# Two whole-row buffers for h in PSUM, borrowed by every other visitor of that memory

## The chip, the cores and the metric

The kernel runs on one core of one Trainium2 chip. Its time is the device time of one launch in microseconds (us), as a median of several runs. Five engines take part: TensorE (PE) multiplies, VectorE (DVE) and ScalarE (ACT) read what PE leaves in PSUM, GpSimd (POOL) works on SBUF alone, and SyncE (SP) issues every DMA. Each engine runs its own list of instructions in the order in which the program was written; it stops at an instruction whose semaphores have not come, and everything behind that instruction on the same engine stops with it.

## The reference

```python
def _attn_ref(x, inducing):                 # x: 4 x 12608 x 128, inducing: 32 x 128
    def mab(q, kv):
        s = scale * (q @ kv.transpose(0, 2, 1))
        s = s - s.max(-1, keepdims=True)
        a = np.exp(s)
        a /= a.sum(-1, keepdims=True) + 1e-09
        return a @ kv
    h = mab(I, x)                           # per batch: 32 rows out of 12608
    return mab(x, h)                        # and back: 12608 rows
def _moe_ref(x, w_in, w_out, g_ln):         # x: 50432 x 128, w_in: 128 x 1024, w_out: 1024 x 128
    h = x @ w_in
    sm = softmax of h over its 1024 columns
    solu = h * sm
    ln = (solu - mean) / np.sqrt(var + 1e-06) * g_ln
    return ln @ w_out
```

All inputs and outputs that the kernel moves are float32, but w_in and w_out, which come as float64 and are rounded on the chip.

## The kernel before, in words

Each of the four batches is cut into 99 tiles of up to 128 rows, 396 in all. The first attention needs all rows of a batch before its result exists, so the program has two passes.

**Pass 1** (`p1`, nine groups of up to 12 tiles per batch) loads rows, turns them on PE (L561, a visit of up to 4 tiles each), copies the turned rows to SBUF on ACT (L547) and stores them for pass 2. It then computes scores (L589), their maxima (DVE L605, PE L614), exponentials (ACT L639) and a weighted sum of the rows (PE L665, "gather"). `combine` closes a batch: the sum of weights (L707), the 32 mean rows (L714), and their product with w_in (L726), kept in SBUF as `hs`.

**Pass 2** (`p2`) loads the turned rows, computes scores against the 32 rows (L768) and turned weights `aT` (L804). `main` then makes each tile's hidden row block `h` = `aT` times `hs` (L902): 128 x 1024 float32, which is two of PSUM's eight banks. The text calls this **mm1**. `soft` follows: DVE scales h, takes its minimum and moves it to SBUF (L940); ACT takes the exponential (L950); POOL multiplies (L954); ACT squares (L965); DVE turns blocks of 32 x 32 (L978). Four tiles make a group. `products` multiplies a group with w_out (L1023); `evacuate` moves the result out of PSUM on DVE or ACT (L1045); `finish` scales the rows (ACT L1100 or POOL L1096) and stores them.

PE's row groups are used apart. The products of a group come as two streams, each of which keeps two of the four row groups busy. A **beat** is one step of PE: both streams side by side (full), one stream and one step of mm1 side by side (full), or one of the three alone (half). mm1 is four beats; one stream is 32.

PSUM before: two banks for h, one buffer alone; two each for the two streams (`op0`, `op1`); one bank `tr` for the turns and scores of `p2` and the turns of `p1`; one bank `pb` for `p1`'s scores and sums. Batch 0's pass 1, the early phase, has nothing beside it and borrows the banks of `op` and h.

The order on every engine comes from a planner in the program (`Planner`), which runs while the program is built. Every operation has a cost in ns and a priority; `AFTER` has the latency between two engines; `Lock` hands out buffers to the tasks that wait, the most urgent first. `driver` emits products in PE's spare time, `JC` beats at a time, and a stream joins if it will be ready within `EAGER` ns. `SWITCH` is what the planner adds for a visit to another use of PE. Where the planner sees PE idle for more than `FILL` ns it writes dummy transposes (L488).

Of the kernel before, what the change touches and what calls it, by code (L numbers as in the profile page):

```python
# [11 lines left out]
U32 = mybir.dt.uint32  # L12
# [17 lines left out]
JC = 1  # L30
BEAT = 225
EAGER = 60
SWITCH = 170


def cut(total, most, unit):
# [28 lines left out]
PR_EV = -60
PR_FI = 20
PR_G2 = 6
PR_HN = -2
PR_MU = -1
PR_SQ = 1.5  # L70
PR_TU = 3
RUSH = -100.0
SLACK = {"PE": 100, "ACT": 0, "DVE": 300, "POOL": 0, "SP": 0}
SPARE = 150
WARM = 32
WOUT = -13.5

AFTER = {
    "PE": {"PE": 0, "ACT": 197, "DVE": 196, "POOL": 200, "SP": 250},
    "ACT": {"PE": 205, "ACT": 143, "DVE": 142, "POOL": 61, "SP": 50},  # L80
    "DVE": {"PE": 256, "ACT": 128, "DVE": 127, "POOL": 155, "SP": 50},
    "POOL": {"PE": 205, "ACT": 75, "DVE": 74, "POOL": 100, "SP": 50},
    "SP": {"PE": 1036, "ACT": 1000, "DVE": 920, "POOL": 1000, "SP": 1000},
# [27 lines left out]
class Lock:  # L111


    def __init__(self, bufs=()):
        self.free = [(b, ()) for b in bufs]
        self.waiting = []


class Planner:
# [18 lines left out]
    def give(self, lock, buf, *after):  # L138
        lock.free.append((buf, after))
        while lock.free and lock.waiting:  # L140
            lock.waiting.sort(key=lambda w: (w[0][1], w[1]))
            task, _ = lock.waiting.pop(0)
            self.blocked -= 1
            self._step(task, lock.free.pop(0))

    def _step(self, task, value):
        gen = task[0]
        while True:
# [90 lines left out]
def set_attention_then_solu_kernel(ctx: ExitStack, tc: tile.TileContext, x, inducing, w_in, w_out, g_ln, out):  # L239
# [21 lines left out]
    psum = pool("psum", 1, PSUM)  # L261
# [29 lines left out]
    op_b = [buf([P, 2, 512], f"op{w}", where=psum) for w in range(2)]  # L291
    op_e = [o[:, i, :] for o in op_b for i in range(2)]
    early_h = tc.tile_pool(name="h_early", bufs=1, space=PSUM, side="right")
    where = early_h.__enter__()
# [8 lines left out]
    H, VT, XN, XT, TRB, PB = (Lock() for _ in range(6))  # L303
# [8 lines left out]
    OS = Lock(bufs(2, [P, GS, C], "os"))  # L312
# [126 lines left out]
    def weights_in():  # L439
        g = yield from rounded(w_in_sb, w_in.bitcast(U32), conv, None, conv_free, -18.5)  # L440
        plan.set(w_in_ready, g)

    def weights_out():
# [30 lines left out]
        give(TRB, mp, d)  # L474
        rows = wc.rearrange("p (k q) d -> p k q d", q=4)
        spread = []
        for a in range(4):
            for q in range(4):
                c = yield dma(
                    M * FF * 4,  # L480
                    lambda: nc.sync.dma_start(rows[a * M : (a + 1) * M, :, q, :C], wg[q * M : (q + 1) * M]), d, issue=600, prio=LATE,
# [10 lines left out]
    def points():  # L492
        def warm():
# [8 lines left out]
        give(TRB, tr_b, d)  # L502
        plan.scratch = (TRB, PB, H)
# [8 lines left out]
    EARLY_X = Lock([spare[:, i * each : (i + 1) * each].rearrange("p (s c) -> p s c", c=C) for i in range(SPARES * FF // each)] + xn_b[:1])  # L512
    EARLY_T = Lock([vt_all[:, i * each : (i + 1) * each].rearrange("p (s t) -> p s t", t=P) for i in range(3 * GS * FF // each)] + [xT_b])
    e2 = xn_b[1].rearrange("p s c -> p (s c)")
    EARLY_EW = Lock([(e2[:, i * 2 * PG * M : (i * 2 + 1) * PG * M], e2[:, (i * 2 + 1) * PG * M : (i + 1) * 2 * PG * M].rearrange("p (s m) -> p s m", m=M)) for i in range(2)] + [ew_b])
    EARLY_TR = Lock(op_e[:3])
    EARLY_PB = Lock([*h_e, pb_b, op_e[3]])
# [3 lines left out]
    def p1(b, k):  # L521
# [4 lines left out]
        lx, lt, ltr, lpb, lew = (EARLY_X, EARLY_T, EARLY_TR, EARLY_PB, EARLY_EW) if early else (XN, XT, TRB, PB, EW)  # L526
# [16 lines left out]

        def copy(c0, c1, tr, d):
# [679 lines left out]
```

## Time and profile before

| | |
|---|---|
| median of 3 runs | 1289.62 us (1284.67 to 1293.36) |
| the profiled execution | 1285.68 us, of which the span from first to last instruction is 1283.9 us |
| busy over the span | PE 97%, PE weight loads 87%, DVE 89%, ACT 89%, POOL 86% |
| granted TensorE clock | 0.992 on average |

A busy share counts the time in which at least one instruction of the engine was in flight. Matmuls overlap each other, so short gaps between them do not show in PE's share. The sum in the prediction is made against 1285.68 us; the median of the runs lies 3.94 us above it.

### The profile page before, as it was taken

The numbers are of one execution on the slowest core, as the hardware profiler recorded it, in microseconds if no ns is written. First come the engines' busy times: TensorE is split into PE (matmuls) and PEld (weight loads), VectorE is DVE, ScalarE is ACT, GpSimd is POOL, SyncE is SP. The second block draws the span as 40 slices with busy tenths as digits, with TensorE's granted clock in tenths as the row PEclk, the third lists the DMA queues.
The fourth block names the chain that finished last, engine by engine and source line by source line (L and its number), as shares of the span: only waits on it lengthen the run. The fifth ranks groups of instructions, "written<-read, shape, count | busy, mean of one in ns | idle before, by whom it ended". The sixth has DMA issues, their size and how long they took to land.

```text
span 1283.9 us, 75837 instructions
## 1 busy us (share of the span) xinstructions
PE 1246.2 (97%) x34221; PEld 1120.8 (87%) x34221; DVE 1140.8 (89%) x1825; ACT 1140.1 (89%) x2418; POOL 1104.2 (86%) x981
## 2 busy tenths in 40 slices
PE   8899999999999999999999999999999999999996
PEld 6689888889888888889888998888989999999996
DVE  5589989999898989999888999899999999999993
ACT  5489999999889989999789999989988999999993
POOL 2388988889889988988888997978889999999994
PEclk9999999999999999999899999999999999999998
DMA  9652333331232233332133134233021211111111
GB/s 361 188 164 70 111 103 94 93 111 43 77 117 60 78 102 119 103 109 74 28 102 94 43 103 138 91 101 102 21 82 54 58 55 53 54 38 43 29 29 41
DMA packets 118149, 113.46 MB, mean 88 GB/s; under 512 B 76577, under 2 KB 83777, under 8 KB 117697
## 3 DMA queue, kind: packets, MB, share of 16 engines
q1 hardware_dynamic: 117824, 108.62, 27.6%
q8 instruction: 267, 4.37, 1.4%
q14 instruction: 58, 0.47, 0.1%
HBM read 54.30 MB, written 52.18 MB: 83 GB/s over the span
## 4 chain that ended last, share of the span: by engine, by line
PE 70%; DVE 3%; ACT 2%; issue 1%; POOL 1%; POOLq 0%; DVEq 0%; ACTq 0%
PE op L1023 46%; PE h L902 15%; PE tr L561 2%; PE tr L804 2%; PE tr L768 1%; PE pb L665 1%; PE pb L589 1%; ACT sq L965 1%; DVE spare L940 1%; DVE vt L978 1%; ACT eu L950 1%; POOL eu L954 1%; PE pb L726 0%; DVE hn L940 0%; PE pb L614 0%
## 5 line engine op out<-in xcount | busy, mean ns | idle before, releaser
L1023 PE MATMUL op<-wc,vt 32*128 32x129 f32 x25600 | 1007.7, 275 | 12.5 <-issue 8.4
L1023 PEld LDWEIGHTS op<-wc,vt 32*128 32x128 f32 x25600 | 945.4, 185 | 54.3 <-issue 39.8
L902 PE MATMUL h<-hs,aT 32*128 32x128 f32 x6336 | 442.8, 277 | 3.2 <-DVE spare L940 1.2
L902 PEld LDWEIGHTS h<-hs,aT 32*128 32x128 f32 x6336 | 387.9, 187 | 32.1 <-DVE spare L940 6.2
L954 POOL TENSOR_TENSOR eu<-spare,eu 128x1024 f32<-128x1024 f32 x144 | 341.2, 2376 | 33.8 <-ACT eu L950 33.4
L954 POOL TENSOR_TENSOR eu<-hn,eu 128x1024 f32<-128x1024 f32 x140 | 331.8, 2376 | 25.1 <-ACT eu L950 24.3
L978 DVE STREAM_TRANSPOSE vt<-eu 128x1024 f32<-128x1024 f32 x284 | 349.2, 1233 | 1.1 <-POOL eu L954 0.9
L965 ACT ACTIVATE sq<-eu 128x1024 bf16<-128x1024 f32 x284 | 298.9, 1053 | 17.2 <-POOL eu L954 13.7
L940 DVE TENSOR_SCALAR_CACHE_REDUCE hn<-h,rn 128x1024 f32<-128x1024 f32 x198 | 252.1, 1273 | 38.8 <-PE h L902 30.6
L940 DVE TENSOR_SCALAR_CACHE_REDUCE spare<-h,rn 128x1024 f32<-128x1024 f32 x198 | 251.8, 1272 | 37.2 <-PE h L902 28.2
L950 ACT ACTIVATE eu<-hn,nm 128x1024 f32<-128x1024 f32 x140 | 160.3, 1145 | 19.9 <-DVE hn L940 19.0
L950 ACT ACTIVATE eu<-spare,nm 128x1024 f32<-128x1024 f32 x144 | 164.9, 1145 | 10.7 <-DVE spare L940 10.5
L954 POOL TENSOR_TENSOR spare<-hn,spare 128x1024 f32<-128x1024 f32 x58 | 137.5, 2374 | 15.6 <-ACT spare L950 15.5
L954 POOL TENSOR_TENSOR spare<-spare 128x1024 f32<-128x1024 f32 x54 | 128.0, 2373 | 16.9 <-ACT spare L950 16.4
L978 DVE STREAM_TRANSPOSE vt<-spare 128x1024 f32<-128x1024 f32 x112 | 138.2, 1235 | 0.0
L965 ACT ACTIVATE sq<-spare 128x1024 bf16<-128x1024 f32 x112 | 117.7, 1051 | 9.3 <-POOL spare L954 8.3
L1100 ACT ACTIVATE os<-spare,fin 128x128 f32<-128x128 f32 (+1 forms) x276 | 86.9, 391 | 1.5 <-POOL fin L1085 1.2
L950 ACT ACTIVATE spare<-hn,nm 128x1024 f32<-128x1024 f32 x58 | 66.4, 1145 | 6.7 <-DVE hn L940 6.4
L1045 DVE COPY spare<-op 128x258 f32<-128x258 f32 (+1 forms) x123 | 50.2, 416 | 24.6 <-PE op L1023 23.6
L950 ACT ACTIVATE spare<-spare,nm 128x1024 f32<-128x1024 f32 x54 | 61.9, 1146 | 6.5 <-DVE spare L940 6.5
L965 ACT ACTIVATION_READ_ACCUMULATOR sq<-eu 128x1 f32 x284 | 54.2, 191 | 0.0
L561 PE MATMUL tr<-ident,xn 128*128 128x128 f32 x297 | 48.8, 287 | 0.4 <-DMA xn<-in_x_dram 0.4
(180 smaller groups left out, 1028.0 us busy)
## 6 DMA issues: line engine op xcount, KB each, us to landing
out_dram<-os SPq DMA_DIRECT2D x96, 256.0 KB, 2.4
xT<-xd SPq DMA_DIRECT2D x27, 768.0 KB, 4.6
xn<-in_x_dram SPq DMA_DIRECT2D x22, 768.0 KB, 5.4
xd<-xT SPq DMA_DIRECT2D x21, 768.0 KB, 4.3
dl<-dd SPq DMA_DIRECT2D x396, 1.0 KB, 2.4
xd<-vt SPq DMA_DIRECT2D x7, 768.0 KB, 10.6
spare<-in_x_dram SPq DMA_DIRECT2D x5, 768.0 KB, 10.3
xT<-xd SPq DMA_DIRECT2D x5, 512.0 KB, 4.2
```

The source lines that it names most:

```text
L561: nc.tensor.transpose(out=tr[:, (s - c0) * P : (s - c0 + 1) * P], in_=xn[:, s, :], identity=ident)
L589: nc.tensor.matmul(sc[g * M : (g + 1) * M, : nn * M], lhsT=indT, rhs=xT[:, :nn, g * M : (g + 1) * M], start=True, stop=True)
L804: nc.tensor.transpose(out=tr[:h, (q - q0) * P : (q - q0 + 1) * P], in_=a4[:, q * P : q * P + h], identity=ident)
L902: nc.tensor.matmul(hp[:, cols], lhsT=aT[rows, i // 2, :], rhs=hs[rows, cols], start=True, stop=True)
L940: lambda: nc.vector.tensor_scalar(out=hn, in0=hp, scalar1=rn, scalar2=None, op0=ALU.mult, op1=ALU.min, accum_out=nm),
L950: "ACT", 1133, lambda: nc.scalar.activation(e, hn, AF.Exp, bias=nm, scale=-1.0, accum_out=G["S"][:, s : s + 1]), d, rel, srel,
L954: d = yield Op("POOL", 2330, lambda: nc.gpsimd.tensor_tensor(out=e, in0=hn, in1=e, op=ALU.mult), de, prio=t + PR_MU)
L965: "ACT", 1040, lambda: nc.scalar.activation(sq, e, AF.Square, scale=1.0 / 32.0, accum_out=G["qe"][:, s, 0:1]), d,
L978: lambda: nc.vector.transpose(out=G["vtb"][:, : n * FF].rearrange("p (j s t) -> p j s t", j=M, s=n)[:, :, s, :], in_=e.rearrange("p (a f) ...
L1023: nc.tensor.matmul(op[:rows, a - 2 * w, : C + 1], lhsT=vt[q, k, :], rhs=wc[q, k, :], start=(k == 0), stop=(k == JB - 1))
L1045: return lambda: eng(F["raw"][:rows, i0 : i0 + 2, :], op[:rows, :, : C + 1])
L1100: nc.scalar.activation(os[:rows, q, :], raw[:, q, :], AF.Copy, scale=y[:, i0 + q : i0 + q + 1])
```

## The change

PSUM now holds two h buffers of two banks each, and the two stream buffers; `tr` and `pb` are gone. Turns, scores, sums of `p1` and `combine`, and the scores and turns of `p2`, each take one of the h buffers from the same lock for their visit and give it back. Since such a buffer is 1024 columns wide, late turns of `p1` go up to 6 tiles a visit instead of 4, those of `p2` up to 8 column blocks instead of 4, and `combine`'s product with w_in is one visit instead of two. The `p1` score visit gives its buffer back after the exponentials, and the gather takes one again.

The early phase has eight banks of its own, four for turns and four for scores, and more places for loaded rows, so that all nine groups of batch 0 have one. The h and stream buffers exist only when that phase and its `combine` are done. The planner's constants change: SWITCH 170 to 400, all latencies between engines in AFTER 80 ns longer, JC 1 to 2, EAGER 60 to 120, and the priorities.

```diff
-JC = 1
+JC = 2
-EAGER = 60
-SWITCH = 170
+EAGER = 120
+SWITCH = 400
+H_LAST = -30
-HN_MORE = 3
+HN_MORE = 4
-FILL = 1200
+FILL = 400
-P1_FROM = 0
-P1_GO = 20
-P1_STEP = 8
-P2_AHEAD = 29
+P1_FROM = 5
+P1_GO = -20
+P1_STEP = 7
+P2_AHEAD = 35
-PR_TU = 3
+PR_TU = 6
...
-    "PE": {"PE": 0, "ACT": 197, "DVE": 196, "POOL": 200, "SP": 250},
+    "PE": {"PE": 0, "ACT": 277, "DVE": 276, "POOL": 280, "SP": 330},
...
-    op_b = [buf([P, 2, 512], f"op{w}", where=psum) for w in range(2)]
-    h_e = [buf([P, 512], f"h_e{i}", where=where) for i in range(2)]
-    tr_b = buf([P, 512], "tr", where=psum)
-    pb_b = buf([P, 512], "pb", where=psum)
+    bank_e = [buf([P, 512], f"bank_e{i}", where=where) for i in range(8)]
...
-    EARLY_TR = Lock(op_e[:3])
-    EARLY_PB = Lock([*h_e, pb_b, op_e[3]])
+    EARLY_TR = Lock(bank_e[:4])
+    EARLY_PB = Lock(bank_e[4:])
...
-        lx, lt, ltr, lpb, lew = (EARLY_X, EARLY_T, EARLY_TR, EARLY_PB, EARLY_EW) if early else (XN, XT, TRB, PB, EW)
+        lx, lt, ltr, lpb, lew = (EARLY_X, EARLY_T, EARLY_TR, EARLY_PB, EARLY_EW) if early else (XN, XT, H, H, EW)
...
+        most = 4 if early else -(-n // 2)
-        for c0 in range(0, n, 4):
-            c1 = min(c0 + 4, n)
+        for c0 in range(0, n, most):
+            c1 = min(c0 + most, n)
...
+        if not early:
+            give(lpb, big, de)
+            big, rel = yield lpb
+        pooled = big[:, 512 - C : 512]
-        dp = yield Op("PE", 74 * n, gather, d)
+        dp = yield Op("PE", 74 * n, gather, d, rel)
...
-        for k in range(2):
-            spawn(half(slice(k * 512, (k + 1) * 512)), PRIO_P1(b, NP - 1))
+        for k in range(1 if b else 2):
+            spawn(half(FF if b else 512), PRIO_P1(b, NP - 1) if b else -28)
...
-        bank = EARLY_TR if b == 0 and j < ON_EARLY else TRB
+        bank = H
-        for q0 in range(0, -(-n // 2), 4):
-            q1 = min(q0 + 4, -(-n // 2))
+        for q0 in range(0, -(-n // 2), 8):
+            q1 = min(q0 + 8, -(-n // 2))
...
-            hp, rel = yield H
+            hp, rel = yield H.at(t + H_LAST)
...
+        bank_pool.__exit__(None, None, None)
+        late = pool("late", 1, PSUM, side="right")
+        for i in range(2):
+            give(H, buf([P, FF], f"h{i}", where=late), *done)
+        plan.scratch = (H,)
+        for w in range(2):
+            give(OP[w], buf([P, 2, 512], f"op{w}", where=late), *done)
```

On PE, in the steady part of the program, before (h_716 is the one h buffer, L902 is mm1, L1023 the products, L561 a turn visit of `p1` into its own bank `tr`):

```order
L1023 MATMUL op1_73<-wc_158,vt_68 128x129 x2
L902 MATMUL h_716<-hs1_126,aT0_95 128x128 x8
L1023 MATMUL op0_72<-wc_158,vt_68 128x129 x2
L1023 MATMUL op1_73<-wc_158,vt_68 128x129 x2
L561 MATMUL tr_79<-ident_139,xn1_71 128x128 x4
L1023 MATMUL op0_72<-wc_158,vt_68 128x129 x2
L1023 MATMUL op1_73<-wc_158,vt_68 128x129 x2
```

Every mm1 writes h_716, so it stands behind DVE's L940 of the tile before it. On PE with the change, one tile's mm1 into h1 and the next tile's into h0 (L924 is mm1, L1045 the products):

```order
L924 MATMUL h1_728<-hs1_125,aT1_96 128x128 x2
L1045 MATMUL op1_730<-wc_157,vt_65 128x129 x2
L924 MATMUL h0_727<-hs1_125,aT1_96 128x128 x2
L1045 MATMUL op0_729<-wc_157,vt_65 128x129 x2
L924 MATMUL h0_727<-hs1_125,aT1_96 128x128 x2
L1045 MATMUL op0_729<-wc_157,vt_65 128x129 x2
L924 MATMUL h0_727<-hs1_125,aT1_96 128x128 x4
L1045 MATMUL op1_730<-wc_157,vt_65 128x129 x12
L924 MATMUL h1_728<-hs1_125,aT1_96 128x128 x8
```

Here two mm1 stand back to back, and the third waits for the first one's buffer. Where a visit holds the other buffer, mm1 stays on one. On PE with the change, a turn visit of `p1` (L571, six tiles) into h0 beside mm1 on h1:

```order
L1045 MATMUL op0_729<-wc_157,vt_65 96x129 x2
L1045 MATMUL op1_730<-wc_157,vt_65 96x129 x2
L571 MATMUL h0_727<-ident_138,xn0_67 128x128 x6
L924 MATMUL h1_728<-hs0_123,aT1_96 128x128 x2
L1045 MATMUL op0_729<-wc_157,vt_65 96x129 x2
L924 MATMUL h1_728<-hs0_123,aT1_96 128x128 x2
```

The visit is longer by two tiles and its buffer comes from the lock of h. On PE at the end of the early phase, before (L665 the last gather, L464 the column means of w_out):

```order
L665 MATMUL h_e0_77<-spare_69,ew_100 32x128 x7
L464 MATMUL tr_79<-hn2_83,ones_mean_151 128x128 x8
L714 MATMUL h_e1_78<-fold_144,accn_137 128x128
L768 MATMUL op1_73<-xT2_87,h4_0_123 32x128 x4
L726 MATMUL pb_80<-w_in_sb_154,h4_0_123 128x512
L726 MATMUL op0_72<-w_in_sb_154,h4_0_123 128x512
L804 MATMUL op1_73<-ident_139,a4_94 128x128 x2
L902 MATMUL h_716<-hs0_124,aT0_95 128x128 x8
```

and with the change (L682 is the gather, L493 the dummy transposes, L731, L747, L790 and L826 what L714, L726, L768 and L804 were):

```order
L682 MATMUL bank_e4_76<-xn1_68,ew_99 32x128 x7
L493 MATMUL bank_e0_72<-ident_138 128x128 x14
L731 MATMUL bank_e2_74<-fold_143,accn_136 128x128
L493 MATMUL bank_e0_72<-ident_138 128x128 x6
L747 MATMUL bank_e3_75<-w_in_sb_153,h4_0_122 128x512
L747 MATMUL bank_e5_77<-w_in_sb_153,h4_0_122 128x512
L790 MATMUL h0_727<-xT2_86,h4_0_122 32x128 x4
L465 MATMUL h0_727<-hn2_82,ones_mean_150 128x128 x8
L826 MATMUL h0_727<-ident_138,a4_93 128x128 x2
L790 MATMUL h1_728<-xT2_86,h4_0_122 32x256 x4
L924 MATMUL h0_727<-hs0_123,aT0_94 128x128 x8
```

The product with w_in moved ahead of the first scores of pass 2, the means of w_out behind them, and 20 dummy transposes stand in the gap.

## Rows read from the trace of the kernel before

**Rows 1.** The page's first part: busy time, share of the span, instructions.

```profile
PE 1246.2 (97%) x34221; PEld 1120.8 (87%) x34221; DVE 1140.8 (89%) x1825; ACT 1140.1 (89%) x2418; POOL 1104.2 (86%) x981
```

**Rows 2.** Stages by windows: length, each engine's busy time (instructions), clock, DMA, GB/s.

```profile
core 0: us, PE busy (x) PEld busy (x) DVE busy (x) ACT busy (x) POOL busy (x), PEclk, DMA share, GB/s
70.00:1000.00 930.00, 913.48 (x25456) 815.88 (x25458) 853.60 (x1368) 853.23 (x1803) 821.33 (x713) 1.00 0.29 88
1000.00:1190.00 190.00, 186.98 (x5570) 175.60 (x5566) 178.50 (x251) 179.56 (x377) 183.82 (x165) 1.00 0.18 49
1190.00:1254.00 64.00, 64.00 (x1953) 62.18 (x1952) 59.84 (x76) 62.41 (x135) 62.81 (x54) 1.00 0.11 28
```

**Rows 3.** The chain that ended last: start, length, what.

```profile
1253.40 20.70 PE op L1023 x644
```

**Rows 4.** Timeline of one tile, 1231.0 to 1233.8 us: start, length, engine, line.

```profile
1231.07 0.38 PE L902 MATMUL h<-hs,aT 32*128 32x128 f32 x2
...
1231.28 0.28 PE L902 MATMUL h<-hs,aT 32*128 32x128 f32 x2
...
1231.97 1.84 PE L1023 MATMUL op<-wc,vt 32*128 32x129 f32 x58
1232.37 1.28 DVE L940 TENSOR_SCALAR_CACHE_REDUCE spare<-h,rn 128x1024 f32<-128x1024 f32 x1 [0.20 <-PE h L902]
...
1233.58 0.08 DVE L940 DVE_READ_ACCUMULATOR spare<-h,rn 128x1 f32 x1
...
1233.72 0.38 PE L902 MATMUL h<-hs,aT 32*128 32x128 f32 x2
```

**Rows 5.** Line L940, 70 to 1000 us: what DVE waited for, us, times.

```profile
  PE h L902: 42.7, 97
```

**Rows 6.** Line L940, 1000 to 1260 us: the same.

```profile
  PE h L902: 10.0, 39
```

**Rows 7.** Line L902, 70 to 1000 us: what idle PE waited for, us, times.

```profile
  DVE spare L940: 6.3, 10
...
  DVE hn L940: 3.7, 6
```

**Rows 8.** Timeline of PE around one visit of four transposes.

```profile
99.57 0.28 PE L902 MATMUL h<-hs,aT 32*128 32x128 f32 x2
...
99.68 0.28 PE L902 MATMUL h<-hs,aT 32*128 32x128 f32 x2
99.89 0.66 PE L804 MATMUL tr<-ident,a 128*128 128x128 f32 x4
100.47 0.95 PE L1023 MATMUL op<-wc,vt 32*128 32x129 f32 x24
```

**Rows 9.** Waits over the span: us, times, longest.

```profile
PE pb L714 <- DVE accn L712: 2.3, 2, 1.9
```

**Rows 10.** Timeline of the end of the early phase.

```profile
43.30 2.19 PE L488 MATMUL tr<-ident 128*128 128x128 f32 x18
...
48.53 0.64 PE L665 MATMUL h_e<-spare,ew 128*32 128x128 f32 x14 [0.30 <-ACT hn L453]
...
52.73 0.42 PE L768 MATMUL op<-xT,h 128*32 128x128 f32 x8 [1.36 <-DVE h L716]
...
53.09 1.13 PE L726 MATMUL pb<-w_in_sb,h 128*128 128x512 f32 x2
...
54.05 1.02 PE L726 MATMUL op<-w_in_sb,h 128*128 128x512 f32 x2
...
55.11 0.59 ACT L728 COPY hs<-op 128x512 f32<-128x512 f32 x1
...
56.35 1.16 PE L902 MATMUL h<-hs,aT 32*128 32x128 f32 x16 [0.46 <-ACT aT L812]
```

**Rows 11.** Line L561, 70 to 1284 us: what idle PE waited for.

```profile
  ACT xT L547: 0.2, 1
```

**Rows 12.** One stage by windows, columns as in rows 2.

```profile
635.00:642.00 7.00, 6.19 (x82) 4.64 (x82) 4.49 (x6) 2.28 (x4) 3.19 (x3) 0.53 0.02 2
```

More of the change, by code (lines that the diff above doesn't have):

```diff
@@ L290, in set_attention_then_solu_kernel @@
     xn_b = bufs(2, [P, PG, C], "xn")
[L291 to L297 removed]
+    bank_pool = tc.tile_pool(name="early", bufs=1, space=PSUM, side="right")
+    where = bank_pool.__enter__()
+    bank_e = [buf([P, 512], f"bank_e{i}", where=where) for i in range(8)]
     hn_b = bufs(3, [P, FF], "hn")
@@ L302, in set_attention_then_solu_kernel @@
     xT_b = buf([C, PG, P], "xT")
-    H, VT, XN, XT, TRB, PB = (Lock() for _ in range(6))
+    H, VT, XN, XT = (Lock() for _ in range(4))
     OP = [Lock(), Lock()]
@@ L473, in weights_out @@
         )
-        give(TRB, mp, d)
+        give(H, mp, d)
+        for k in range(NP):
+            yield p1_done[0][k]
+        o = yield Op("POOL", 200, lambda: nc.gpsimd.memset(wc[:, :, C : C + 1], 1.0), [d for e in p1_done[0] for d in e.after])
+        o_end = [o]
         rows = wc.rearrange("p (k q) d -> p k q d", q=4)
@@ L613, in p1 @@
         )
-        d = yield Op("PE", SWITCH + 110, lambda: nc.tensor.matmul(mq, lhsT=fold2, rhs=v["mdiag"], start=True, stop=True), d)
+        d = yield Op("PE", (80 if early else SWITCH) + 110, lambda: nc.tensor.matmul(mq, lhsT=fold2, rhs=v["mdiag"], start=True, stop=True), d)
         first = k == 0
@@ L721, in combine, with half, rows @@
         done = []
-        def half(part):
+        def half(width):
             hp, prel = yield bank
-            d = yield Op(
-                "PE", 857, lambda: nc.tensor.matmul(hp, lhsT=h4, rhs=w_in_sb[:, part], start=True, stop=True), dh, prel, w_in_ready.after
-            )
-            d = yield Op("ACT", 478, lambda: nc.scalar.copy(hs[:, part], hp), d, rel)
+            at = len(done) * width
+            done.append(None)
+            def rows():
+                for k in range(0, width, 512):
+                    nc.tensor.matmul(hp[:, k : k + 512], lhsT=h4, rhs=w_in_sb[:, at + k : at + k + 512], start=True, stop=True)
+            d = yield Op("PE", 857 * width // 512, rows, dh, prel, w_in_ready.after)
+            d = yield Op("ACT", 52 + 426 * width // 512, lambda: nc.scalar.copy(hs[:, at : at + width], hp[:, :width]), d, rel)
             give(bank, hp, d)
-            done.append(d)
-            if len(done) == 2:
+            done[at // width] = d
+            if None not in done and len(done) * width == FF:
                 plan.set(hw_ready[b], *done)
-        for k in range(2):
-            spawn(half(slice(k * 512, (k + 1) * 512)), PRIO_P1(b, NP - 1))
+        for k in range(1 if b else 2):
+            spawn(half(FF if b else 512), PRIO_P1(b, NP - 1) if b else -28)
     aT_of = {(b, j): {"all": Event()} for b in range(NB) for j in range(len(at_groups[b]))}
@@ L1149, in handover @@
             done += d
+        d = yield hw_ready[0]
+        done += d
+        bank_pool.__exit__(None, None, None)
[5 more added lines that the diff above has]
+            give(OP[w], buf([P, 2, 512], f"op{w}", where=late), *done)
+        for k in range(NP):
             d = yield xd_done[(0, k)]
             done += d
-        d = yield hw_ready[0]
-        done += d
-        early_h.__exit__(None, None, None)
-        give(H, buf([P, FF], "h", where=pool("h", 1, PSUM, side="right")), *done)
-        give(PB, pb_b, *done)
         wide = 4 * FG * (C + 1)
@@ L1166, in handover @@
         give(XT, xT_b, *done)
+        for o in os_b:
+            give(OS, o, *done)
         give(EW, ew_b, *done)
```

99 lines of the change are left out of this document (48 added, 51 removed).

## The prediction

> **What bounds the kernel now.** I read the page's first part, then the stages by windows, then the chain of waits, and last the lines that make and read h. The page alone shows four engines near 90% and PE at 97% [rows 1]. The windows tell stages apart [rows 2]. From 70 to 1000 us, where pass 1 of the next batch runs beside pass 2, DVE and ACT are busy 853 of 930 us (92%), POOL 821 (88%), PE 913 (98%). From 1000 to 1190 us, when little of pass 1 is left, POOL has 183.8 of 190 us (97%), and from 1190 to 1254 us 62.8 of 64 (98%). So the last quarter has no room on POOL, which the change does not touch; room is in the first three. The chain ends with 20.7 us of nothing but products on PE [rows 3]: at the close PE is behind, and what shortens PE's list shortens the end.
>
> The tile's timeline shows the loop through the one h buffer [rows 4]. mm1 starts at 1231.07, DVE takes h at 1232.37 and is done with it at 1233.65 (1232.37 + 1.28), and the next mm1 starts at 1233.72: 2.65 us for a tile, in which nothing but this loop has to wait. PE's own content of that tile is 4 beats of mm1 and 7 of products (the row of 58 records, eight to a full beat). Its beats take 0.223 us: mm1's later steps stand 0.11 us apart, two to a beat [rows 8]. 11 x 0.223 = 2.45 us, so PE loses 0.195 us here. Half of that shows as the first step of mm1, which takes 0.21 us (1231.07 to 1231.28) in place of 0.11. DVE waited for h 97 times from 70 to 1000 us, 42.7 us in all [rows 5], and 39 times after that, 10.0 us [rows 6]. PE stood fully idle for DVE's L940 only 6.3 + 3.7 us [rows 7], since its in-flight matmuls hide the rest.
>
> **The change, part by part.** The sum is on PE, because PE's list is what runs without a break from the first mm1 to the last product.
>
> *The loop through h.* In the new order 213 of 395 mm1 go to the other buffer than the one before them. Of the 182 that stay on a buffer, 2 have seven beats or fewer and no visit between them and their forerunner; before it was 131 of 395. So this wait goes nearly everywhere: 97 x 0.195 = -18.9 us up to 1000 us. The bounds are 10 us (what shows as idle [rows 7]) and 42.7 us (all of DVE's wait [rows 5]). I take the tile's own loss, since both engines meet there. After 1000 us POOL has 7.4 us of room left in 254 [rows 2], so 39 such stalls can give back little: -2.
>
> *Fewer, longer visits.* The order has 79 turn visits of pass 1 in place of 100, 37 of pass 2 in place of 64, and in the later batches 3 visits with w_in in place of 6: 51 fewer. A visit of four transposes ends the beats at 99.79 (last step at 99.68 + 0.11), and the products' first step is at 100.47 [rows 8], with that step 0.1 us slow to follow, as after any stop. Of these 0.68 us four transposes at 0.109 (half of a beat each) are 0.44, and the visit itself costs 0.25. 51 x 0.25 = -12.8 us. The ACT copies grow with their visits and hide beside PE.
>
> *More half beats.* Counted in the order, PE has 4228 beats before and 4288 now, since JC and EAGER let a stream run alone more often. 60 x 0.223 = +13.4 us. All of them lie before the last batch, 3046 there before and 3108 now.
>
> *The start.* Before, the last gather starts at 48.53 and the first mm1 at 56.35 [rows 10]. Of this, 52.73 to 56.35 (3.6 us) is the chain of pass 2's first visit. Now the gather (0.64) is followed by 14 dummy transposes at 0.12 (18 took 2.19) = 1.7, the turn of the mean rows 0.4, 6 more dummies 0.7, both products with w_in 2.0, their copy 0.6 and then the same 3.6: 9.6 against 7.8 us, +1.8. Ahead of it stand 92 dummy transposes where there were 69, +2.8 us, while all x of batch 0 is loaded without a break, which takes waits out of pass 1. I set these two against each other; the bounds are -5 and +3.
>
> *The wait for the mean rows.* PE stood 2.3 us at L714 [rows 9]. The change puts over 40 rows between the sum of weights and that product where there were 7 to 17, and the other h buffer is free meanwhile: -2.3.
>
> *The new wait.* 188 late visits now ask for an h buffer: 27 groups of pass 1 with two turns, a score and a gather each, 37 of pass 2 with two, and two for each of three combinations. Behind a visit that waits on PE stand the products, and behind those DVE's and ACT's L1045. Before, a bank of their own made them wait hardly ever: turns 0.2 us, once [rows 11]. No row shows a visit that waits for L940. The nearest is mm1 doing so, 0.195 us. From below the cost is nothing, since in the order at least 1.8 us of PE work stands between an mm1 and nearly every visit that follows on its buffer, against 1.28 + 0.2 us for DVE; from above it is 0.195 at each of the 188, 36.7 us. I take one in ten, +3.7, nearer the lower end because of that distance.
>
> DVE loses 23 of its 123 evacuations to ACT; neither is on the path that I sum, so it counts nothing; were PE not the bound, this would help DVE, which is level with ACT.
>
> *Against the change.* The granted clock is 1.00 over the 930 us as a whole [rows 2], but 0.53 from 635 to 642 us [rows 12], which is 1.2 of 2.4 GHz for nearly all of it and comes right after the stop at L714. Such a stretch costs about half its length, 3.3 us. The Trainium skill ("TensorE: Matmul & The Clock Gate", on psum-queue depth-cycling) tells of a kernel that cycled through PSUM buffers in every iteration and idled between groups so often that the clock kept falling and rising. By it this change could add such stretches; one more per batch would make my sum 13 us longer. The trace has cycling through the two stream buffers without it, so I add none.
>
> Sum: -18.9 - 2 - 12.8 + 13.4 + 1.8 - 2.3 + 3.7 = **-17.1 us**, 1268.6 us against the profiled 1285.68. With the 3.9 us by which the median lies higher, **1272 us**, 1.3% faster.
>
> **The rivals.**
>
> *A, the vector engines were the bound and PE only kept them company.* For it: DVE's idle time from 70 to 1000 us is 76 us, and 42.7 of it is the wait for h. Then that wait comes back whole, -42.7 and -2, and the PE terms do not count: 1289.6 - 45 = **1245 us**. Against it: PE's list has no slack that DVE could use, and half beats have grown. The Trainium skill ("Perfetto Trace Analysis", Identifying the Most-Contended Engine) holds matmul occupancy for a poor measure and would have PE judged by its weight loads, 87% over the span [rows 1] and 88% from 70 to 1000 us [rows 2], below DVE and ACT; by that rule A is right. Chance 0.27.
>
> *B, PE's content is all that counts.* Only the fully idle 10 us come back [rows 7], a quarter of the visits wait (+9.2), and the rest stands: -10 - 12.8 + 13.4 + 1.8 - 2.3 + 9.2 = -0.7, **1289 us**. The change would then do what it says in the buffers and nothing in the time. For it: 1.8% of PE's time is all that is not covered from 70 to 1000 us [rows 2]. Chance 0.20.
>
> *C, slower: PE stands at the visits.* L571, L600, L682, L790 and L826 wait in PE's list for a buffer that DVE has not read yet, because L940 has queued behind a turn of 1.2 us; products and mm1 of the other buffer stand behind them. At 0.195 us for each of the 188 it is +36.7 in place of +3.7: 1272 + 33 = **1305 us**. It decides from about 0.18 us a visit, where the sum passes 1% above 1289.6. Against it is the distance in the order. Chance 0.12.
>
> **How the numbers follow.** The forecast has 0.41, with a range of its own of 1260 to 1284. About 1% is what a measurement of this kernel can tell from no change, 1276.7 to 1302.5 us here. Faster: all of A and two thirds of the forecast, 0.27 + 0.27 = 0.54. Same: B, the rest of the forecast and a little of C, 0.36. Slower: 0.10. The range of 1242 to 1298 leaves out the faster half of A (0.1) and most of C (0.1).
>
> **What would show it.** In the profile after, L962 should wait for mm1 far less than 42.7 us up to 1000 us, and mm1 for L962 hardly at all. The first step of mm1 should be 0.11 us nearly always. PE's weight loads should rise above 88% from 70 to 1000 us. The first mm1 should start 0 to 4 us later than 56.35. If A holds, DVE and ACT pass 95% there. If C holds, waits of PE on L962 stand at the visits' lines. The forecast is wrong if mm1 waits less and the products wait more instead, for turned tiles (L1000) or for L1067.

## The result, and the profile after

The changed kernel takes **1269.5 us** (median of 4 runs, 1267.48 to 1270.31); the kernel before took 1289.6 in the same runs. The ratio is 0.985, with a 95% interval of 0.983 to 0.987, which is clear of 1. The forecast was 1272 us, so the time came out as summed. Several of its terms did not, and two reasons were wrong.

The profiled execution has a span of 1265.6 us, against 1283.9: 18.3 less. The page's first part, and then the same stages by windows as in [rows 2], the last one up to 1236 us:

```profile
PE 1236.0 (98%) x34240; PEld 1127.8 (89%) x34240; DVE 1123.3 (89%) x1803; ACT 1141.3 (90%) x2402; POOL 1100.9 (87%) x977
```

```profile
70.00:1000.00 930.00, 920.50 (x25768) 834.65 (x25768) 850.51 (x1364) 862.97 (x1803) 824.37 (x717) 0.99 0.30 90
1000.00:1190.00 190.00, 188.06 (x5803) 181.28 (x5805) 180.79 (x252) 186.64 (x394) 186.60 (x163) 1.00 0.16 41
1190.00:1236.00 46.00, 45.63 (x1467) 44.75 (x1466) 42.29 (x57) 45.08 (x98) 45.16 (x41) 1.00 0.13 34
```

Beside [rows 1, 2]: from 70 to 1000 us PE's weight loads go from 816 to 835 us (88 to 90%) while DVE stays where it was (854, now 851). More tiles pass in the same time, and DVE loses evacuations to ACT. From 1000 to 1190 us ACT and POOL are both at 98%.

The rows that answer to [rows 5, 6], what DVE waits for before it takes h at L962, first 70 to 1000 us, then 1000 to 1260 us:

```profile
  PE h L924: 29.1, 48
```

```profile
  PE h L924: 1.3, 2
```

From 42.7 us to 29.1, and from 10.0 to 1.3. PE's own idle time ahead of mm1, from 70 to 1000 us, the rows beside [rows 7]:

```profile
  DVE spare L962: 5.4, 6
  DVE hn L962: 2.5, 4
```

7.9 us in place of 10.0. A visit with six transposes, timeline of PE, beside [rows 8]:

```profile
86.35 0.28 PE L924 MATMUL h<-hs,aT 32*128 32x128 f32 x2
86.37 0.28 PE L1045 MATMUL op<-wc,vt 32*128 32x129 f32 x2
86.57 0.87 PE L571 MATMUL h<-ident,xn 128*128 128x128 f32 x6
87.38 1.27 PE L1045 MATMUL op<-wc,vt 32*128 32x129 f32 x34
```

The beats end at 86.48 (86.37 + 0.11) and the products' first step is at 87.38: 0.90 us, of which six transposes at 0.109 are 0.65. The visit itself is 0.25 us, as before with four. The product with the mean rows (beside [rows 9]; the number behind the second bar is the idle time) waits 0.3 us in place of 2.3, and the first mm1 starts at 56.32, not later than 56.35 in [rows 10]:

```profile
L731 PE MATMUL h<-fold,accn 128*128 128x128 f32 x6 | 1.5, 326 | 0.3 <-DVE accn L729 0.3
```

```profile
56.32 1.02 PE L924 MATMUL h<-hs,aT 32*128 32x128 f32 x14
```

The clock, windows with the columns of [rows 2]: first the stretch after the first mm1 in the kernel before, then the same stretch and two later ones in the changed kernel. [rows 12] had 0.53 from 635 to 642 us:

```profile
57.00:81.40 24.40, 23.02 (x247) 18.78 (x247) 17.99 (x29) 15.26 (x31) 15.99 (x13) 0.86 0.90 210
```

```profile
57.00:81.40 24.40, 18.44 (x178) 13.86 (x175) 18.33 (x29) 14.35 (x27) 17.44 (x13) 0.51 0.88 214
600.00:640.00 40.00, 40.00 (x1188) 37.92 (x1192) 37.88 (x56) 36.13 (x73) 38.93 (x34) 1.00 0.29 84
640.00:700.00 60.00, 59.08 (x1772) 55.75 (x1768) 56.21 (x87) 56.08 (x119) 57.12 (x54) 1.00 0.28 83
```

The low stretch behind the stop at the combination is gone with that stop. The one near the start is longer: the clock is at its lower level (0.50, 1.2 GHz) for 24 us, where it was for 7. In these 24 us the kernel before puts 59 dummy transposes between its first mm1, and PE is busy 23.0 us; the changed kernel has none there, and PE is busy 18.4. The first mm1 starts at the same time in both, but that of tile 24 at 131.4 us in place of 129.4.

Last the longest pieces at the end of the chain of waits, beside [rows 3] (start, length, what):

```profile
1229.72 7.42 PE op L1045 x244
1237.14 3.21 PE h L493 x28
1240.35 7.36 PE op L1045 x256
1248.62 7.28 PE op L1045 x256
```

The last mm1 is 26 us earlier (1226.3 against 1252.2), but from it to the end it takes 39.3 us against 31.7: PE still has these products, and 28 dummy transposes among them.

**PE's ledger.** PE's stops can be read off the start times of its matmul records. Two steps in a row stand 0.11 us apart; a gap is what two successive starts have above 0.112 us, if that is over 0.02. The sums from about 55 us, just ahead of the first mm1, to the end, in us (number of gaps), sorted by what stands on either side (a gap between a turn visit and another visit counts with the turn visits):

```
                          before       after       e4          e7          e8          e2          e9
product -> mm1         17.8 (216)   6.2 ( 60)  12.7 ( 94)   7.8 ( 84)   7.6 ( 72)  13.7 (143)  34.1 (201)
mm1 -> mm1              5.6 ( 55)  10.3 ( 53)  10.0 ( 46)   8.2 ( 42)  10.2 ( 65)  28.4 (151)  49.7 (182)
mm1 -> product          5.0 ( 15)   3.7 ( 10)   3.4 ( 11)   7.3 ( 16)   2.1 ( 11)  13.2 ( 46)  25.5 ( 76)
product -> product     29.6 (242)  25.4 (251)  28.2 (251)  28.8 (257)  38.5 (282)  28.2 (265)  46.5 (521)
turn visits            36.4 (401)  23.9 (275)  35.6 (414)  25.4 (273)  25.5 (281)  23.8 (272)  37.2 (293)
other visits           51.1 (317)  53.4 (345)  55.6 (340)  56.8 (347)  56.7 (342)  57.8 (345)  67.1 (347)
dummy transposes        2.6 ( 20)   0.5 (  6)   0.0         1.0          0.5         0.0         0.0
all                   148.1        123.4       145.6       135.3       141.0       165.3       260.0
of these at 1.2 GHz     9.7         16.0        14.7        18.9        22.2        38.7        81.9
```

The last row is needed to read the others. At 1.2 GHz two steps stand 0.215 us apart (mm1 at 77.86, 78.08 and 78.29 us in the changed kernel), so each such step counts as a gap though PE did not stop. Of the mm1 to mm1 gaps, 1.4 of 5.6 us lie there before, 7.8 of 10.3 after, 21.1 of 28.4 in e2.

e2 to e9 are the experiments below; each column is of one profiled execution. From the first mm1 to PE's last step it is 1217.4 us before and 1199.3 after, 18.1 less; the gaps of that stretch give back 24.3, and 24 dummy transposes fewer 2.7. What is left, the content, went up by 9; it is a remainder and was not measured by itself.

### The profile page after: what moved, and what is told of

It reads as the page before. It is cut to its first block, busy times and chain, and to the rows that moved or that the text cites. A ratio compares the mean times of both kernels' runs of the same rounds, so it can differ in the third digit from the quotient of the medians.

```text
span 1265.6 us, 75903 instructions
## 1 busy us (share of the span) xinstructions
PE 1236.0 (98%) x34240; PEld 1127.8 (89%) x34240; DVE 1123.3 (89%) x1803; ACT 1141.3 (90%) x2402; POOL 1100.9 (87%) x977
## 5 line engine op out<-in xcount | busy, mean ns | idle before, releaser
L1045 PE MATMUL op<-wc,vt 32*128 32x129 f32 (+1 forms) x25600 | 1000.0, 274 | 6.6 <-issue 2.9
L1045 PEld LDWEIGHTS op<-wc,vt 32*128 32x128 f32 (+1 forms) x25600 | 944.3, 185 | 59.1 <-issue 44.3
L976 POOL TENSOR_TENSOR eu<-spare,eu 128x1024 f32<-128x1024 f32 x187 | 442.2, 2373 | 37.5 <-ACT eu L972 37.3
L924 PE MATMUL h<-hs,aT 32*128 32x128 f32 x6336 | 432.0, 275 | 6.4 <-DVE spare L962 3.2
L1000 DVE STREAM_TRANSPOSE vt<-eu 128x1024 f32<-128x1024 f32 x330 | 406.6, 1236 | 27.8 <-POOL eu L976 26.5
L924 PEld LDWEIGHTS h<-hs,aT 32*128 32x128 f32 x6336 | 389.4, 188 | 21.4 <-DVE spare L962 5.9
L987 ACT ACTIVATE sq<-eu 128x1024 bf16<-128x1024 f32 x330 | 347.0, 1051 | 39.9 <-POOL eu L976 33.4
L976 POOL TENSOR_TENSOR eu<-hn,eu 128x1024 f32<-128x1024 f32 x143 | 338.3, 2374 | 30.8 <-ACT eu L972 28.3
L962 DVE TENSOR_SCALAR_CACHE_REDUCE spare<-h,rn 128x1024 f32<-128x1024 f32 x226 | 283.1, 1257 | 24.0 <-PE h L924 19.8
L962 DVE TENSOR_SCALAR_CACHE_REDUCE hn<-h,rn 128x1024 f32<-128x1024 f32 x170 | 213.4, 1258 | 15.8 <-PE h L924 13.6
L972 ACT ACTIVATE eu<-spare,nm 128x1024 f32<-128x1024 f32 x187 | 213.5, 1142 | 7.1 <-DVE spare L962 6.8
L976 POOL TENSOR_TENSOR spare<-spare 128x1024 f32<-128x1024 f32 x39 | 92.6, 2375 | 3.9 <-ACT spare L972 3.9
L1000 DVE STREAM_TRANSPOSE vt<-spare 128x1024 f32<-128x1024 f32 x66 | 81.7, 1237 | 6.4 <-POOL spare L976 5.9
L987 ACT ACTIVATE sq<-spare 128x1024 bf16<-128x1024 f32 x66 | 69.4, 1051 | 7.3 <-POOL spare L976 5.9
L976 POOL TENSOR_TENSOR spare<-hn,spare 128x1024 f32<-128x1024 f32 x27 | 64.1, 2374 | 7.1 <-ACT spare L972 7.1
L1067 DVE COPY spare<-op 128x258 f32<-128x258 f32 (+1 forms) x100 | 40.9, 414 | 19.4 <-PE op L1045 18.2
L571 PE MATMUL h<-ident,xn 128*128 128x128 f32 x297 | 44.3, 283 | 0.3 <-ACT aT L834 0.3
L1067 ACT COPY spare<-op 128x258 f32<-128x258 f32 (+1 forms) x100 | 35.8, 363 | 8.7 <-PE op L1045 6.7
## 6 DMA issues: line engine op xcount, KB each, us to landing
spare<-in_x_dram SPq DMA_DIRECT2D x5, 768.0 KB, 12.8
```

The source lines that it names most:

```text
L571: nc.tensor.transpose(out=tr[:, (s - c0) * P : (s - c0 + 1) * P], in_=xn[:, s, :], identity=ident)
L924: nc.tensor.matmul(hp[:, cols], lhsT=aT[rows, i // 2, :], rhs=hs[rows, cols], start=True, stop=True)
L962: lambda: nc.vector.tensor_scalar(out=hn, in0=hp, scalar1=rn, scalar2=None, op0=ALU.mult, op1=ALU.min, accum_out=nm),
L972: "ACT", 1133, lambda: nc.scalar.activation(e, hn, AF.Exp, bias=nm, scale=-1.0, accum_out=G["S"][:, s : s + 1]), d, rel, srel,
L976: d = yield Op("POOL", 2330, lambda: nc.gpsimd.tensor_tensor(out=e, in0=hn, in1=e, op=ALU.mult), de, prio=t + PR_MU)
L987: "ACT", 1040, lambda: nc.scalar.activation(sq, e, AF.Square, scale=1.0 / 32.0, accum_out=G["qe"][:, s, 0:1]), d,
```

## The experiments

All times are medians; the kernel before had 1289 to 1290 us in each set of runs. All experiments change the changed kernel (1269.5 us) unless another is named. Planner numbers that aren't shown are the changed kernel's.

**e4, short visits again.**

```
-        most = 4 if early else -(-n // 2)
+        most = 4
-        for q0 in range(0, -(-n // 2), 8):       (q1 likewise)
+        for q0 in range(0, -(-n // 2), 4):
```

> The changed kernel with turn visits of at most four transposes, as before the change: 48 visits more (21 of pass 1, 27 of pass 2), everything else the same; 4283 beats against 4288. Theory L (a visit costs PE 0.25 us and PE is the path): 48 x 0.25 = +12, less 1: 1280 us. By the gaps of the two traces (31.4 us at turn visits before, 20 after, 102 visits against 53... 0.22 each) +10.5: 1279 us. Rival A (vector engines or POOL bound the time): within 2 us of the changed kernel, 1268 to 1272 us. Rival C (a turn of 1.2 us holds products up): 1260 to 1267 us.

Measured 1285.3 us, ratio to the kernel before 0.997 (0.995 to 0.998): 15.8 us more than the changed kernel. The profiled execution was the slowest of eleven, with a span 21.9 us longer. In its ledger the turn visits are back at 35.6 us, from 23.9, which is 11.7 of that and what theory L priced (the expectation's 31.4 and 20 us are 36.4 and 23.9 here); product to mm1 takes 6.5 more. Rival A, by which PE's visits would cost nothing, falls. ACT has more to do as well: its copies of turned tiles (L557, L834) take 73.3 us in place of 66.3. But from 70 to 1000 us it is busy 844 us in place of 863, so it waited more and did not set the time:

```profile
70.00:1000.00 930.00, 913.42 (x25115) 815.80 (x25117) 834.31 (x1337) 843.89 (x1794) 802.99 (x700) 0.99 0.29 89
```

**e1, one h buffer for mm1, the other for all visits.**

```
+    HM = Lock()
-            hp, rel = yield H.at(t + H_LAST)
+            hp, rel = yield HM.at(t + H_LAST)
...
-            give(H, buf([P, FF], f"h{i}", where=late), *done)
+            give((H, HM)[i], buf([P, FF], f"h{i}", where=late), *done)
```

(Also the gather and the combination wait for the gather before them ahead of taking the one visit buffer, since they would lock each other out.)

> The changed kernel, but of its two h buffers one is for mm1 alone and the other for all visits (turns, scores, sums, combinations), so mm1 has one buffer again, as before, and no visit ever takes mm1's. The order has 4328 beats, 40 more than the changed kernel. Theory L (the loop through h is what the second buffer took away, and it is paid on PE): the 40 beats give +8.9 us, the loop gives back +11.6 (the gaps ahead of mm1 after a product are 17.8 us in the kernel before and 6.2 in the changed one) to +18.9 (what the prediction summed): 1290 to 1297 us. Rival B (only PE's content counts): +8.9, 1278 us. Rival C (visits that share mm1's buffers cost more than the loop): 1260 to 1268 us. The wait of DVE's L962 for mm1 from 70 to 1000 us should be near 43 us again by L, near 29 by B.

Measured 1407.8 us, ratio 1.092 (1.090 to 1.094). Far outside of all three. The order has 836 dummy transposes, since the planner believes PE idle all the time, so this run can't price the loop. The next ones take it apart.

**e9, the same without those dummies.** FILL 400 becomes 4000.

> The first run once more (mm1 on one h buffer, all visits on the other, the numbers of the changed kernel), but FILL 4000, so that the planner puts in no dummy transposes where it believes PE idle: 71 in place of 836, 4326 beats. Theory D (those dummies, 765 at 0.12 = 92 us, stood on PE's path and made most of the first run's 138 us): 1300 to 1322 us. Rival W (they filled time in which PE waited for h anyway): above 1370 us.

Measured 1423.8 us, ratio 1.103 (1.100 to 1.106): 16 us *slower* than with them. Rival W holds: they filled time in which PE waits. What idle PE waits for ahead of mm1, 70 to 1000 us (L928 is mm1 here, L966 DVE's h):

```profile
  DVE spare L966: 29.9, 32
  DVE hn L966: 24.2, 26
```

54 us in place of 7.9, and in the ledger every kind of gap between mm1 and products has grown (82 of its 260 us lie at 1.2 GHz, 16 of 123 in the changed kernel). Over the whole span DVE in its turn waited for mm1, too (us of idle time behind the second bar, of two rows of the page):

```profile
L966 DVE TENSOR_SCALAR_CACHE_REDUCE spare<-h,rn 128x1024 f32<-128x1024 f32 x226 | 285.7, 1264 | 47.8 <-PE h L928 39.2
L966 DVE TENSOR_SCALAR_CACHE_REDUCE hn<-h,rn 128x1024 f32<-128x1024 f32 x170 | 215.2, 1266 | 60.7 <-PE h L928 52.3
```

So with one buffer and these numbers, PE and DVE wait for each other in turn.

**e3, the kernel before with the changed kernel's numbers**, nothing else.

```
-JC = 1
-EAGER = 60
-SWITCH = 170
+JC = 2
+EAGER = 120
+SWITCH = 400
...
-    "PE": {"PE": 0, "ACT": 197, "DVE": 196, "POOL": 200, "SP": 250},
+    "PE": {"PE": 0, "ACT": 277, "DVE": 276, "POOL": 280, "SP": 330},
...
```

> The kernel before (one h buffer, banks of their own for turns and sums, short visits) with the planner's numbers of the changed one. 4308 beats against 4228 of the kernel before. Theory L: 80 beats at 0.223 us give +17.8: about 1307 us, in any case no faster than 1289. Rival N (the numbers made the gain): 1268 to 1278 us.

Measured 1409.4 us, ratio 1.092 (1.090 to 1.095). Rival N falls, and theory L missed by 100 us; the order has 997 dummies.

**e10, the same with FILL 4000.**

> The third run once more (the buffers of the kernel before, the numbers of the changed one) with FILL 4000: 32 dummy transposes in place of 997, 4324 beats against 4228 before. Theory D: 1409 - 965 x 0.12 = 1293, and with 96 half beats at 0.223 against the kernel before 1289.5 + 21 = 1311: 1293 to 1315 us. Rival N (without the dummies the numbers alone carry the gain): 1268 to 1280 us. Rival W: above 1370 us.

Measured 1416.7 us, ratio 1.097 (1.094 to 1.100). Rival W again: with the buffers of before, these numbers cost 127 us.

**e2, the changed kernel with the numbers of before**, the reverse of e3.

> The changed kernel's buffers and visits with the planner's numbers of the kernel before (JC 1, EAGER 60, SWITCH 170, the old AFTER table, SLACK, FILL, HN_MORE, P1 and P2 starts and the priorities). 4294 beats against 4288. Theory L (buffers and visits made the gain, the numbers only rearrange): 1268 to 1276 us. Rival N (the numbers, above all 80 ns more lag in AFTER, made the gain): 1284 to 1290 us, as before the change.

Measured 1311.7 us, ratio 1.017 (1.015 to 1.018). Neither theory: two shared buffers with the old numbers are 22 us *slower* than the kernel before. Idle PE ahead of mm1 (70 to 1000 us), and the stage around the first change of batch by windows:

```profile
  DVE hn L962: 19.4, 19
  DVE spare L962: 18.0, 25
```

```profile
260.00:350.00 90.00, 89.74 (x2492) 81.24 (x2491) 84.57 (x144) 83.49 (x181) 74.00 (x68) 1.00 0.30 93
350.00:390.00 40.00, 40.00 (x943) 33.34 (x935) 18.05 (x47) 21.60 (x55) 15.19 (x21) 1.00 0.40 137
390.00:480.00 90.00, 86.00 (x2139) 78.61 (x2138) 80.62 (x123) 80.71 (x162) 79.56 (x64) 0.91 0.22 67
```

From 350 to 390 us DVE is busy 18 of 40 us. PE's products go on (30 of its 40 us), beside them pass 1 of the next batch is made up, and mm1's only instructions in these 40 us (count; duration ns min/median/max; first and last start) come at the very end (the clock then falls, 0.91 in the next row):

```profile
L924 PE MATMUL h<-hs,aT x16: 270/270/372, 388.4 to 389.3; 32*128 32x128 f32 x16
```

**e6, e2 with P1_GO -20 in place of 20.**

> The second run (shared buffers, the numbers of before) with one number of the changed kernel: P1_GO -20 in place of 20, so that a visit of pass 1 gets an h buffer ahead of an mm1 that is 10 tiles further on, not 50. In the second run each batch's last third and the change of batch stand still: mm1 of tiles 66, 165 and 264 to 99, 198 and 297 take 137, 142 and 127 us, 93, 94 and 98 in the changed kernel, while the first two thirds are faster there. 4347 beats. Theory S (visits starve for a buffer, pass 1 ends late): the three stretches come back to 95 to 105 us each and the whole to 1270 to 1288 us. Rival (the lags in AFTER, mm1 put too close to what it waits for: gaps between two steps of mm1 sum to 24.5 us there and 5.2 in the changed kernel): stays at 1300 to 1312.

Measured 1297.4 us, ratio 1.005 (1.004 to 1.007): 14.2 us less than e2. The three stretches took 106, 98 and 95 us: theory S holds for the stall. The stage of 350 to 390 us is now as busy as any other, its row from 280 us on, and idle PE ahead of mm1 waits less:

```profile
280.00:386.00 106.00, 104.94 (x3009) 96.88 (x3003) 98.52 (x148) 99.43 (x210) 100.47 (x87) 1.00 0.24 68
```

```profile
  DVE spare L962: 6.0, 9
  DVE hn L962: 6.0, 8
```

But the whole missed theory S's range by 9 us, and 28 us to the changed kernel are left. They are not waits at full clock: counted as in the ledger from the first mm1 on, those sum to 101 us in e6 and 107 in the changed kernel. The profiled execution has 22 us more of gaps at 1.2 GHz, where its clock stays from 53 to 121 us, and 13 us more content (4347 beats against 4288). PE, which waits 8 us in the stretch shown, is at the lower level throughout:

```profile
56.00:121.00 65.00, 57.32 (x471) 45.95 (x473) 45.24 (x75) 40.52 (x75) 37.38 (x28) 0.50 0.43 118
```

**e5, one h buffer for mm1 and one for visits, with the numbers of before.**

> One h buffer for mm1 and the other for all visits, as in the first run, but with the planner's numbers of the kernel before, whose dummy transposes and half beats fit one buffer: 4277 beats, 144 dummy transposes (836 in the first run, 160 before the change). Against the kernel before this has the longer visits and one place for all visits in place of two. Theory L: 1289.5 - 12 for the visits + 49 beats x 0.223 (+11) + some waits of visits for each other: 1288 to 1295 us, so 20 us of the changed kernel's gain come from mm1 having both. Rival C' (visits that share a buffer with mm1 cost what the loop gave, and the longer visits made the gain): 1268 to 1280 us. Rival N (the numbers fit neither): 1305 or more, as the second run.

Measured 1300.1 us, ratio 1.007 (1.005 to 1.010), 5 us above theory L's range. DVE's wait for mm1 is where it was in [rows 5, 6], first 70 to 1000 us, then 1000 to 1300 us:

```profile
  PE h L928: 50.4, 96
```

```profile
  PE h L928: 11.2, 38
```

With both buffers and the same numbers (e2) it is 30.7 us from 70 to 1000 us. So one buffer for mm1 makes that wait, whatever the visits' length and banks. Fewer, longer visits did not make this faster than the kernel before. With the old numbers splitting is 11.5 us *faster* than sharing (e2), and 2.7 us slower once P1_GO is -20 (e6).

**e7, JC 1 and EAGER 60. e8, the AFTER table of before.**

> The changed kernel with JC 1 and EAGER 60 as before the change. The prediction laid its 60 extra beats to these two; but with the old values the order has 4328 beats, 40 more than the changed kernel's 4288. Theory L (a beat is 0.223 us of PE and PE is the path): +8.9, 1278 us. Rival A (a half beat fills time in which PE would wait for the vector engines): 1266 to 1272 us.

> The changed kernel with the old AFTER table (80 ns less between an engine's end and the start of what waits for it on another engine). 4311 beats, 23 more: +5.1 us by the beats. Theory L: nothing else changes, 1272 to 1277 us. Rival N (instructions stand too close behind what they wait for, and the in-order queues pass each wait on): 1280 to 1300 us, with DVE and PE waiting more for each other than in the changed kernel (mm1 to mm1 gaps 10 to 25 us in place of 5.2).

Measured 1287.5 us for e7, ratio 0.998 (0.997 to 1.000), and 1290.1 for e8, ratio 1.001 (0.999 to 1.002): 18.0 and 20.6 us more than the changed kernel, either of them nearly the whole gain. e7 is 9.5 us beyond theory L; for e8 rival N's time holds, but not its place: mm1 to mm1 gaps stay at 10.2, as in the changed kernel (10.3 in the same count). It is the products that lose. Their rows of the page (busy time, mean ns; idle time), of the changed kernel, e7 and e8:

```profile
L1045 PE MATMUL op<-wc,vt 32*128 32x129 f32 (+1 forms) x25600 | 1000.0, 274 | 6.6 <-issue 2.9
```

```profile
L1045 PE MATMUL op<-wc,vt 32*128 32x129 f32 x25600 | 1015.4, 275 | 14.0 <-issue 9.0 <-DVE vt L1000 2.3 <-ACT spare L1067 0.8
```

```profile
L1045 PE MATMUL op<-wc,vt 32*128 32x129 f32 (+1 forms) x25600 | 1016.8, 275 | 15.4 <-issue 12.3 <-ACT spare L1067 2.5
```

The same 25600 products keep PE busy 15 to 17 us longer and have it idle 7 to 9 us longer. In the ledger e8 has 13.1 us more between products. DVE waits less for mm1 in both, 22.7 us in e7 and 22.2 in e8 from 70 to 1000 us in place of 29.1, though both are slower. From the first mm1 to PE's last step, e7's profiled execution is 24.4 us longer than the changed kernel's, 11.8 of it gaps and 12.5 content; of e8's 27.6 us, 17.2 are gaps and 10.3 content.

**e11, POOL does half of its work in the last batch.** `e[:, :part]`, `hn[:, :part]`, with part = 512 for the last batch; the other half of the product is left out.

> The changed kernel, in the last batch (tiles 297 to 395) POOL multiplies only half the columns of a tile; the other half of the product is left out. The order of every engine is the same. POOL loses about 99 x 1.2 us. Theory P (POOL, 98% busy there, sets the pace of the last batch): the time falls until PE's content is left, whose gaps in the last batch sum to 13 us, and the end by 8 more: 1245 to 1256 us. Theory L (PE sets the pace, POOL only the last 20 us, in which products wait for its last tiles): -5 to -9, 1260 to 1265 us. Neither: 1268 to 1271.

Measured 1265.3 us, ratio 0.981 (0.979 to 0.984); the interval overlaps the changed kernel's. The stage of 1000 to 1190 us by windows:

```profile
1000.00:1190.00 190.00, 188.06 (x5831) 181.81 (x5825) 180.68 (x254) 187.37 (x397) 112.81 (x163) 1.00 0.17 45
```

POOL is 74 us less busy than in the changed kernel's row, and PE, DVE and ACT are busy to 1 us as before; the instruction counts are the same to 1%. From tile 297 to the end it took 297.1 us against 300.1. POOL's 98% were no bound: theory P falls. ACT is at 98% there too, and no run relieved it. From the last mm1 to the end it took 38.8 us (39.3 with a whole POOL).

**e12, four of the last ten multiplications on DVE.** `alt=Op("DVE", 1180, ...)` at L976 for t >= 386, a try for a faster kernel.

> The changed kernel, but four of the last ten tiles are multiplied on DVE in place of POOL (the planner may choose for these ten). After the last mm1 the changed kernel needs 39.3 us to its end, the kernel before 31.7, because POOL still has eight tiles at 2.4 us ahead of it while DVE waits 1.1 us for it at each turn. Theory P/L: POOL is through up to 9 us earlier, PE's own work after the last mm1 is some 27 us, so 4 to 8 us come back: 1261 to 1266 us. Rival (PE's products are the end anyway): 1268 to 1271 us.

Measured 1273.3 us, ratio 0.987 (0.984 to 0.989): no gain that can be told. The tail after the last mm1 shrank to 32.0 us, but the last mm1 came 14.3 us later; 4.8 of these were there at tile 386, ahead of the edit. From 1236 to 1246 us POOL is down to 7.2 of 10 us, and PE is busy throughout:

```profile
1236.00:1246.00 10.00, 10.00 (x304) 9.88 (x301) 9.56 (x14) 9.95 (x22) 7.21 (x4) 1.00 0.27 84
```

The rival holds: relieving POOL at the end, here and in e11, does not move the end. That the end is PE's list is argued from that; why mm1 fell behind (the four multiplications stand in DVE's queue ahead of h) is argued, too. No version beat the changed kernel by more than can be measured.

## Why the prediction was right, and where it was wrong

*That PE's list is the path: right.* Visits cost at least what PE pays for them (e4), and halving POOL's work in the last batch moved the median by 4.2 us, with intervals that overlap (e11). Rival A is out: from 70 to 1000 us DVE is at 91% and ACT at 93%, under the 95% that it called for, while e4, which gives PE 48 more visits and ACT 7 us more of copies, costs 15.8 us and leaves ACT less busy there. By the Trainium skill ("Perfetto Trace Analysis", Identifying the Most-Contended Engine) ACT (93%) would come before PE's weight loads (90%) there; the runs show PE's order as what costs time. For the last batch that is argued: POOL is ruled out there, ACT is not.

*The loop through h: right in kind, too large.* Predicted -20.9 in both stages; product to mm1 gaps fell from 17.8 to 6.2 us, **-11.6**. The prediction counted DVE's 97 waits at 0.195 us each up to 1000 us; PE had 216 such gaps over the whole span, of 0.08 us on average. The tight loop of [rows 4] was the wrong row to price them by. The stages were the wrong way round, too: up to tile 297 these gaps fell from 10.7 to 5.7 us, where -18.9 was summed, and from there on from 7.1 to 0.5, where -2 was. DVE's wait fell by 22.3 us, not "far less than 42.7" in the first stage. The first step of mm1 is 0.11 us (under 0.14) in 301 of 396 tiles, 188 before: not nearly always. e5 beside e2 shows that DVE's wait belongs to the one buffer. The sign that was to refute the forecast, products that wait more instead, did not come: from 70 to 1000 us they waited 7.9 us for L1067 and 0.6 for L1000, where it was 7.6 and 2.0.

*Visits: right.* Turns -12.5 and w_in -1.8, **-14.3** for a predicted -12.8; e4 gave the turns' share back. The 0.25 us is the same with six transposes as with four: over all late turn visits the ledger has 0.26 us a visit before and 0.25 after. How much falls to turns depends on the sorting: before, 13 turn visits stood right behind a score visit, with 4.0 us of gaps that count as turns; after, none did. All visits together went from 87.5 to 77.3 us, -10.2, where -11.4 was summed for visits, mean rows and new wait.

*The mean rows: right.* Predicted -2.3, combinations -2.4.

*The new wait: not shown.* Predicted +3.7. Scores, matches, sums and gathers went from 40.5 to 47.0 us, **+6.5**, but 4.0 of that can be the sorting just named. The waits of PE in the profile after have none at a visit's line that ended with L962; for another visit's copy on ACT it stood idle 0.3 us once at L571 and 0.3 once at L682. Rival C is out.

*The start: predicted +1.8, measured 0.*

*Half beats: this step failed.* It put +13.4 us, "since JC and EAGER let a stream run alone more often". PE's content grew by 9 us only, and with the old JC and EAGER (e7) the order has 40 *more* beats and takes 18 us more. So these two numbers do not add the beats. Nor does the count of beats give the time: e8 has 23 more than the changed kernel, 5 us by that price, and takes 20.6 us more. The numbers were not a cost beside the buffers; they are what lets the buffers pay. The medians, us:

```
                                         numbers of before     numbers of the change
own banks, one h (before)                1289.6                1409.4  (few dummies: 1416.7)
one h for mm1, one for the visits        1300.1                1407.8  (few dummies: 1423.8)
two shared h, long visits                1311.7                1269.5
```

The buffers alone cost 22 us, the numbers alone 120; together they give 20. A sum over parts, each costed against the old order, can't see this. That the total fit was partly luck: the loop gave 9 us less than summed, and mm1 to mm1 gaps, most of them at 1.2 GHz, took 4.7 that no term had; the half beats cost 4.5 less, and products among themselves (-4.2) and dummies with their gaps (-4.8), which no term had foreseen either, made up for most of the rest.

*After 1000 us: predicted -2, for a reason that was wrong.* From tile 297 to the end (its mm1 979.9 us before, 965.5 after) it took 304.0 us and then 300.1: -3.9. The ground given, POOL at 97 to 98%, falls with e11, and the gaps ahead of mm1 there gave 6.6.

*Clock: put at nothing, which was right for the steady part and wrong for the start.* The prediction added no low stretch for two buffers in turn. In the changed kernel the granted clock is 0.988 over the span, the low stretch at 635 us is gone, and from 82 us on none comes before the last product. So what the Trainium skill ("TensorE: Matmul & The Clock Gate", on psum-queue depth-cycling) tells of did not happen here. But the 24 us at 1.2 GHz behind the first mm1, where dummy transposes stood before, bring the gaps at that level from 9.7 to 16.0 us, which no term had. That the missing dummies are why is argued; the last section has two pairs of runs that differ in FILL alone.

Open: which of the numbers breaks the one-buffer order of e9 and e10 (no run tried them one by one there), and why AFTER and JC/EAGER each bring nearly all of the gain; the products are where it shows. The table's times hold the clock as well: the profiled executions had 0.988 in the changed kernel, 0.969 in e2, 0.982 in e5, 0.973 in e1 and 0.992 in e3, and no run held it fixed.

## What to carry to other kernels

Where a planner sets the order, its numbers and its buffers are one change: try new buffers with numbers fitted to them, and undo one at a time before any is called a cost or a gain. Price a stop by the gaps in the engine's own start times, over all of its instances, and not by its worst place; look at the clock of those starts first, since a slow step looks like a stop. An engine at 98% is not yet the bound: take some of its work away and see.

## What the hardware showed that was not expected

Dummy transposes that PE makes while it waits kept its clock up. Mean granted clock by slices of the span (40 equal slices, tenths of full speed), first e1 with 836 dummies, then e9 with 71:

```profile
PEclk9969999999999999999999999999999999999999
```

```profile
PEclk9679999998999999999999999999999989989988
```

Over the span it is 0.973 and 0.934. The kernel without them, with less for PE to do, is 16 us slower; the gaps of PE in it, from the first mm1 on, sum to 258 us, against 183 with the dummies, and 82 and 37 of these lie at 1.2 GHz. The other pair says the same: e3 with 997 dummies has 0.992, e10 with 32 has 0.944 and is 7 us slower.
